# The first MLP product on half the rows: blocks of four F tiles, two tiles side by side in two banks, b1 as a bias of the GELU

## The chip, the core and the metric

The kernel runs on one core of a Trainium2 chip. A core has a matrix engine (PE, with its weight loads shown apart as PEld), a vector engine (DVE), a scalar engine (ACT), a general engine (POOL) and a queue processor (SP) that issues most transfers. They run beside each other, each takes its own instructions strictly in order, and they wait for each other by semaphores. Matmul results go to PSUM, eight banks of 512 fp32 columns for each of 128 partitions. The metric is the device time of one execution in microseconds (us).

## The reference

`x` is 2048 rows of 448 values. The result is `x + s * silu(m)`, with two branches that both start from the layer norm of `x`:

- `s` is a diagonal complex state-space model: inputs go through a complex 448 x 448 matrix, a recurrence over the 2048 rows, and a second complex matrix, plus a skip term.
- `m` is an MLP on a second layer norm: `gelu(y @ w1 + b1) @ w2 + b2`, with `w1` of 448 x 1792 and `w2` of 1792 x 448.

```
def _B_ref(x, w1, b1, w2, b2):
    y = _layernorm(x, axis=-1)
    h = _gelu(jnp.einsum("bsd,df->bsf", y, w1) + b1)
    return jnp.einsum("bsf,fd->bsd", h, w2) + b2
```

All inputs and the output are bf16.

## The kernel before

**Tiling.** The 2048 rows are taken in four groups `g` of 512. A group has two blocks `b` of 256 rows, and in each block the even and the odd rows (`par`) are apart, 128 each. The 1792 columns of `w1` are 14 F tiles of 128, loaded in chunks of 4, 4, 4 and 2 tiles (`CH`). `D` = 448 is three and a half times 128, so the contraction of the first product takes four matmuls for each F tile, the last with 64 rows of `w1` only. The other 64 rows of that last piece hold zeros, but for one row: it holds `b1`, and the transposed input has a 1 in that place. So the product comes with its bias.

**First product.** `mm1` (L686) makes two F tiles for a whole group: 2 x 4 matmuls of 128 x 128 weights on 512 columns, into banks 0 and 1 or banks 2 and 3 by turns; one GELU on ACT (L692) reads both banks, 1024 columns. In group 0, `mm1_half` (L701, GELU L707) does the same for one block at a time, with 256 columns, over three pairs of banks (0-1, 2-3, 4-5). The results, `gT`, are the weights of the second product.

**The rest.** `mm2` (L715) multiplies `gT` by `w2`, 14 matmuls of 448 columns; then DVE adds `b2` (L718), ACT takes Tanh (L719), DVE makes `g_sb` (L720). `bu` (L616) makes the inputs of the recurrence in bank 4, ACT copies them out (L620). `ssm` turns them by tables `WT` (Sin, L553, made once), scans them on DVE (L641), ACT copies the scans to bf16 (L645), DVE turns them back into `h_sb` (L669 to L673). `ym` (L747, L750, L753) multiplies `h_sb`, and for even rows the normalized input too, by the output matrices; DVE multiplies by `g_sb` (L756), adds the skip term (L759), and SP stores. `m0` (L605, L607) and `cq` (L566 to L569) make constant matrices once; `lb` (LB0 to LB6, same lines) makes rows that SP transposes as BT0 to BT6, which `bu` reads. `skips` makes four diagonal matrices De0 to De3; they read the GELU of F tile 4, so that they come after it. `ln_stats`, `ln_scale` and `ln_apply` normalize (xn for the recurrence, xm for the MLP); `xt` transposes, by SP (L83) or, at the start, by PE (L440).

**Order.** Nothing is scheduled at run time. Each helper call adds a task with names that it reads and writes; `link` derives the dependences, buffers and banks by name included. The list `ORDER` gives the order in which tasks are put on their engines' queues, and `SECOND` names the tasks that take their second engine. `emit` puts a wait ahead of a task for each dependence, on its own engine's counter too: a task that adds to a bank which an earlier PE task wrote waits for that one's end.

Of the kernel before, what the change touches and what calls it, by code (L numbers as in the profile page):

```python
# [7 lines left out]
ACT = mybir.ActivationFunctionType  # L8
ALU = mybir.AluOpType
BF = dt.bfloat16  # L10
F32 = dt.float32
# [24 lines left out]
class Plan:  # L36
# [33 lines left out]
    def either(self, first, second, reads=(), writes=(), prio=0.0, chain=False):  # L70

        t = self.add(first[0], first[1], reads, writes, chain=chain)
        t.alts.append((second[0], second[1] if isinstance(second[1], list) else [second[1]]))
        return t
# [72 lines left out]
0 9 18 22 10 1 19 23 11 16 15 12 89 2 20 24 3 8 17 21 14 25 13 5 27 26 7 90 6 28 4 91 29 97 46 92 30 98 31 93 99 32 94 47 100 49 95 33 48 50 96 54 104  # L147
101 34 51 102 55 53 103 56 35 63 106 115 52 36 57 107 117 108 64 116 37 109 65 110 38 66 58 119 118 105 39 59 121 120 67 40 123 146 111 122 112 41 125
145 149 124 147 61 45 143 113 62 148 144 60 182 127 73 126 114 42 150 156 129 155 70 154 128 68 153 69 131 157 130 71 72 161 168 133 83 183 158 77 132
74 160 135 75 170 134 76 84 171 137 78 136 79 159 186 81 174 139 169 80 82 138 175 141 86 87 140 85 312 273 88 162 184 310 152 311 142 309 185 314 315  # L150
313 277 316 274 163 317 164 151 165 281 318 166 319 172 278 320 167 321 322 173 285 323 176 279 177 275 280 178 276 180 234 286 282 287 195 43 369 181
235 179 283 192 288 371 284 370 194 373 44 289 372 292 324 193 325 290 375 293 196 327 374 188 328 399 377 198 376 200 201 294 187 204 379 378 199 291
421 202 425 381 419 380 423 402 420 236 424 382 422 197 426 203 427 383 205 237 206 208 207 209 210 387 532 536 431 384 190 220 385 221 391 432 388
224 386 389 211 428 225 212 222 329 392 228 429 395 223 393 189 213 229 226 394 430 437 227 438 214 433 232 230 238 215 231 191 233 216 529 239 533
531 479 535 217 242 243 240 326 480 244 481 241 252 248 218 482 251 249 434 330 250 435 530 219 485 534 331 247 537 390 254 332 396 245 397 246 253
483 486 268 256 257 262 258 333 541 489 263 542 264 484 267 265 266 259 255 260 269 334 261 538 490 539 487 270 540 335 271 398 272 339 295 488 338
340 491 296 297 346 336 492 348 298 345 337 344 497 436 299 347 343 300 302 350 352 353 498 301 354 355 341 543 356 499 342 357 349 400 493 363 351
509 364 358 500 505 359 544 494 360 361 303 545 362 401 304 495 365 305 496 506 501 366 439 507 367 306 368 508 307 405 403 502 503 504 440 406 404
512 408 441 547 548 407 442 409 546 410 412 411 510 443 607 511 444 413 415 445 449 446 549 416 577 447 448 308 450 579 578 453 458 550 580 457 417
581 513 551 451 610 414 452 418 552 459 582 514 455 468 583 456 553 469 470 454 461 471 472 462 554 463 460 464 465 466 585 467 584 473 555 474 587  # L160
586 475 559 556 588 589 476 477 557 558 478 515 560 590 565 566 595 516 564 517 567 518 596 561 597 562 591 569 519 571 598 520 522 568 521 608 592
563 593 609 599 570 594 523 524 572 603 573 574 600 525 575 601 576 604 616 526 605 602 613 606 527 611 528 617 612 620 614 618 615 628 619 621 624
629 622 630 625 623 626 631 627
""".split()]
SECOND = [int(k) for k in """
44 143 144 148 150 168 172 174 178 180 198 200 204 220 230 232 289 290 317 328 402 404 429 434 435 438 511 512 513 538 539 541 542 544 545 607 611 630
# [12 lines left out]
def bass_recurrent_scan__ssm_conv_s5__mixer_channel_mlp__prompt_kernel(  # L179
# [18 lines left out]
    with ExitStack() as es:  # L198
# [22 lines left out]
        De = SB("De", [128, 4, 128])  # L221
        dbc = SB("dbc", [128, D])
# [51 lines left out]
        with nc.Block():  # L274
# [18 lines left out]
            dve(lambda e: e.memset(w1_sb[64:128, 3, :], 0.0), [], ["w1b"], 0.5, S0)  # L293
            dve(lambda e: e.memset(xn2_sb[:].rearrange("p b (r c) -> p (b r) c", r=2)[:, :, D:512], 0.0), [], XM, 0.1, S0)
            dve(lambda e: e.memset(xn2_sb[:].rearrange("p b (r c) -> p (b r) c", r=2)[:, :, D:D + 1], 1.0), XM, XM, 0.1, S0)
# [21 lines left out]
            def ldw1(c, prio):  # L317
                a, w = CH[c][0] * 128, CH[c][1] * 128
                ld("sp", w1_sb[:, 0:3, a:a + w], dram_ap(B_w1, a, [[F, 128], [128 * F, 3], [1, w]]), [f"w1_{c}"], 384 * w * 2, prio, dur=0.55)
                ld("sp", w1_sb[0:64, 3, a:a + w], dram_ap(B_w1, 384 * F + a, [[F, 64], [1, w]]), [f"w1r_{c}"], 64 * w * 2, prio)  # L320
# [6 lines left out]
            ld("sp", w1_sb[64:65, 3, :], dram_ap(B_b1, 0, [[F, 1], [1, F]]), ["w1b"], 4000, S1 + 1)  # L327
# [8 lines left out]
            ld("pool", b2bc[:], dram_ap(B_b2, 0, [[0, 128], [1, D]]), ["b2bc"], 114688, -50, reads=["sgn3", "w1r_3"])  # L336
# [28 lines left out]
            def first_norm():  # L365

                for par in range(2):
# [9 lines left out]
                    dve(lambda e, src=src, dst=dst, mean=mean, r1=r1: e.tensor_scalar(dst, src, mean, r1, op0=ALU.subtract, op1=ALU.mult),  # L377
# [492 lines left out]
```

## Time and profile before

| | |
|---|---|
| time, median of 3 runs | 160.48 us (159.83 to 160.59) |
| profiled execution, first to last instruction | 159.2 us |
| PE busy | 151.3 us, 95% |
| DVE busy | 136.9 us, 86% |
| ACT busy | 93.2 us, 59% |
| first product: L686, L701 matmuls | 38.2 us (168 of 379 ns), 12.9 us (112 of 273 ns) |
| GELU: L692, L707 | 21.4 us (21 of 1021 ns), 8.3 us (14 of 590 ns) |
| second product: L715 | 43.8 us (224 of 352 ns) |
| scans: L641 | 15.6 us (21 of 784 ns) and 4.4 us (7 of 672 ns) |

The mean time of a matmul in a group row runs from its start to its modelled end, and matmuls overlap; what a matmul costs in a dense row of them is the distance from one to the next, which the chain in order of time gives (a piece's length by its count). A busy time is a share of the span; what a stage is worth is read from the chain of work that ended last, which lists for each moment the instruction or transfer that the end was waiting for. The span is from the first to the last instruction; the time of an execution is a little longer.

### The profile page before, as it was taken

How to read it: one execution, taken by the hardware profiler on the slowest of the kernel's cores; microseconds unless marked ns; L12 is line 12 of the kernel's file. 1: busy time of each engine (PE TensorE's matmuls, PEld its weight loads, DVE VectorE, ACT ScalarE, POOL GpSimd, SP SyncE). 2: the span in 40 equal slices, each digit the busy share in tenths (PEclk: the TensorE clock that was granted, in tenths of full speed). 3: DMA queues.
4: the chain of work that ended last, by engine and by line, in shares of the span. 5: the costliest groups of instructions: out<-in, count | busy, mean ns of one | idle time of the engine just before them, and what ended most of it. 6: DMA issues, size and time to landing. Idle time of an engine off the chain costs nothing.

```text
span 159.2 us, 2725 instructions
## 1 busy us (share of the span) xinstructions
PE 151.3 (95%) x946; PEld 93.7 (59%) x946; DVE 136.9 (86%) x265; ACT 93.2 (59%) x151; POOL 51.5 (32%) x127
## 2 busy tenths in 40 slices
PE   6959999999999999999999999999989999999990
PEld 6849965565565556566655555576556655555560
DVE  5478969999998799999789999893999599999982
ACT  3839899997779962689835472212456972450200
POOL 5578840007616000038600573302015420060021
PEclk9999999999999999999999999999999999999998
DMA  4999999888980057000210430213401000010032
GB/s 103 260 303 364 315 149 198 139 161 159 276 172 4 0 100 147 0 0 4 48 20 0 120 65 1 57 21 94 116 4 58 0 4 0 0 58 0 0 115 60
DMA packets 31174, 14.70 MB, mean 92 GB/s; under 512 B 24693, under 2 KB 30713, under 8 KB 31162
## 3 DMA queue, kind: packets, MB, share of 16 engines
q1 hardware_dynamic: 30914, 14.26, 39.4%
q0 software_dynamic: 96, 0.23, 0.4%
q8 instruction: 7, 0.11, 0.3%
q10 hardware_dynamic: 152, 0.05, 0.1%
q14 instruction: 5, 0.04, 0.1%
HBM read 6.89 MB, written 1.84 MB: 55 GB/s over the span
## 4 chain that ended last, share of the span: by engine, by line
PE 88%; DMA 7%; SPq 2%; DVE 1%; issue 0%
PE psum L715 27%; PE psum L686 21%; PE psum L616 13%; PE psum L747 12%; PE psum L701 7%; PE psum L750 4%; DMA w_sb<-in_B_w_dram 4%; PE psum L605 3%; DMA xnT<-xn_sb 3%; SPq L84 2%; PE psum L753 1%; PE psum L440 0%; DVE t L756 0%; DVE tmp L759 0%; PE psum L607 0%
## 5 line engine op out<-in xcount | busy, mean ns | idle before, releaser
L715 PE MATMUL psum<-w_sb,gT 128*128 128x448 bf16 x224 | 43.8, 352 | 0.0
L686 PE MATMUL psum<-xn2T,w_sb 128*128 128x512 bf16 x168 | 38.2, 379 | 0.1
L715 PEld LDWEIGHTS psum<-w_sb,gT 128*128 128x128 bf16 x224 | 21.9, 98 | 20.0
L692 ACT ACTIVATE gT<-psum 128x1024 bf16<-128x1024 f32 x21 | 21.4, 1021 | 11.7 <-PE psum L686 11.6
L686 PEld LDWEIGHTS psum<-xn2T,w_sb 128*128 128x128 bf16 x168 | 18.5, 112 | 15.8 <-issue 0.7
L616 PE MATMUL psum<-xnT,BT 128*128 128x256 bf16 x196 | 24.0, 273 | 0.5 <-DMA xnT<-xn_sb 0.5
L616 PEld LDWEIGHTS psum<-xnT,BT 128*128 128x128 bf16 x196 | 19.0, 98 | 5.8 <-DMA xnT<-xn_sb 1.0
L719 ACT ACTIVATE th<-o 128x448 f32<-128x448 f32 x16 | 9.1, 573 | 16.4 <-DVE o L718 16.3
L641 DVE TENSOR_TENSOR_SCAN s_f<-cw,cur,v_sb 128x256 f32<-128x256 f32 x21 | 15.6, 784 | 0.2
L701 PE MATMUL psum<-xn2T,w_sb 128*128 128x256 bf16 x112 | 12.9, 273 | 2.0 <-DMA w_sb<-in_B_w_dram 1.8
L701 PEld LDWEIGHTS psum<-xn2T,w_sb 128*128 128x128 bf16 x112 | 11.8, 112 | 2.8 <-DMA w_sb<-in_B_w_dram 2.0
L620 ACT ACTIVATE u_sb<-psum 128x512 bf16<-128x512 f32 x12 | 7.2, 596 | 10.2 <-PE psum L616 10.0
L731 POOL TENSOR_TENSOR xd<-xn_sb,dbc 128x448 bf16<-128x448 bf16 x4 | 4.8, 1198 | 24.9 <-DVE dbc L339 13.9
L747 PE MATMUL psum<-CZ,h_sb 128*128 128x448 bf16 x56 | 11.9, 352 | 0.0
L756 DVE TENSOR_TENSOR t<-psum,g_sb 128x448 bf16<-128x448 f32 (+2 forms) x17 | 9.9, 589 | 1.7 <-PE psum L750 1.1
L358 DVE BATCH_NORM_STATS2 lnst<-x_all 128x6 f32<-128x448 bf16 x14 | 8.2, 611 | 3.5 <-DMA x_all<-in_A_x_dram 3.5
L720 DVE SCALAR_TENSOR_TENSOR g_sb<-th,o 128x448 bf16<-128x448 f32 x16 | 10.4, 664 | 0.7 <-ACT th L719 0.6
L718 DVE TENSOR_TENSOR o<-psum,b2bc 128x448 f32<-128x448 f32 x16 | 9.7, 614 | 1.3 <-PE psum L715 1.3
L747 PE MATMUL psum<-CQ,h_sb 128*128 128x448 bf16 (+2 forms) x54 | 10.5, 332 | 0.0
L731 POOL TENSOR_TENSOR xr<-xd,g_sb 128x448 f32<-128x448 bf16 x5 | 5.5, 1106 | 14.6 <-DVE tmp L759 14.5
L707 ACT ACTIVATE gT<-psum 128x512 bf16<-128x512 f32 x14 | 8.3, 590 | 3.2 <-PE psum L701 2.9
L731 POOL TENSOR_TENSOR xr<-x_all,xr 128x448 f32<-128x448 bf16 x6 | 6.9, 1156 | 9.2 <-DVE xr L732 9.1
(157 smaller groups left out, 224.8 us busy)
## 6 DMA issues: line engine op xcount, KB each, us to landing
out_dram<-tmp SPq DMA_DIRECT2D x7, 224.0 KB, 2.0
w_sb<-in_B_w_dram SPq DMA_DIRECT2D x3, 448.0 KB, 7.0
x_all<-in_A_x_dram SPq DMA_DIRECT2D x3, 448.0 KB, 4.4
w_sb<-in_B_w_dram SPq DMA_DIRECT2D x3, 384.0 KB, 6.2
gT<-in_A_C_re_dram SPq DMA_DIRECT2D x1, 392.0 KB, 11.6
Bn<-in_A_B_re_dram SPq DMA_DIRECT2D x1, 336.0 KB, 6.5
Bn<-in_A_B_im_dram SPq DMA_DIRECT2D x1, 336.0 KB, 6.4
gT<-in_A_C_im_dram SPq DMA_DIRECT2D x1, 336.0 KB, 12.0
```

The lines of the kernel that those rows point to most:

```text
L616: fns = [lambda e, r=r, m=m, d=d: e.matmul(psum[:, 4, r * NK:(r + 1) * NK], BT[:, m, d, :], xnT[:, gx, d, :], start=(d == 0), stop=(d == 6 ...
L641: dve(lambda e, i=i, ri=ri, init=init: e.tensor_tensor_scan(s_f[:, i, ri, :], col(R2, i).to_broadcast([128, NK]), v_sb[:, i, ri, :], init, ...
L686: fns = [lambda e, k=k, d=d: e.matmul(psum[:, b0 + k, :], w1_sb[:, d, fcol(2 * j + k)], rhs[:, d, :, :], start=(d == 0), stop=(d == 3)) fo ...
L692: act(lambda e: e.activation(gT[:, gb, 2 * j:2 * j + 2, :], psum[:, b0:b0 + 2, :], ACT.Gelu_apprx_tanh), [f"ps{b0}", f"ps{b0 + 1}"] + (WK ...
L701: fns = [lambda e, k=k, d=d: e.matmul(psum[:, banks[k], :].rearrange("p (r c) -> p r c", r=2)[:, :, cs], w1_sb[:, d, fcol(2 * j + k)], rhs ...
L715: fns = [lambda e, fi=fi: e.matmul(psum[:, bk, 0:D], gT[:, gb, fi, q * 128:(q + 1) * 128], w2_sb[:, fi, :], start=(fi == 0), stop=(fi == N ...
L718: dve(lambda e: e.tensor_tensor(o2[:, fb, :], psum[:, bk, 0:D], b2bc[:], ALU.add), [f"ps{bk}", "b2bc"], [f"oo{fb}"], 0.62, prio - 76)
L719: act(lambda e: e.activation(th[:, fb, :], o2[:, fb, :], ACT.Tanh, scale=0.5), [f"oo{fb}"] + (WK + WKP if g == 0 else []), [f"th{fb}"], 0. ...
L720: dve(lambda e: e.scalar_tensor_tensor(out=g_sb[:, gs, :], in0=th[:, fb, :], scalar=1.0, in1=o2[:, fb, :], op0=ALU.add, op1=ALU.mult), [f" ...
L731: kb.either(("pool", lambda e, o=o, i0=i0, i1=i1, op=op: e.tensor_tensor(o, i0, i1, op), 1.37, 0.15), ("dve", lambda e, o=o, i0=i0, i1=i1, ...
L747: fns = [lambda e, k=k: e.matmul(psum[:, bk, c0:c1], h_sb[:, hb, k, k0:k0 + 128], cm[:, k, c0:c1], start=(k == 0), stop=False) for k in ra ...
L756: dve(lambda e: e.tensor_tensor(t3[:, fb, c0:c1], psum[:, bk, c0:c1], g_sb[:, gs, c0:c1], ALU.mult), [f"ps{bk}", f"g{gs}"], [f"t3{fb}_{c0} ...
```

## The change

**What is computed how.** The zero rows and the row of `b1` go. The last 64 rows of `w1` are loaded twice, into both halves of the partitions, and the last 64 normalized columns are written twice (`ln_apply`, `first_norm`), so that both halves of the fourth piece hold the same 64 rows. Now an F tile is seven matmuls on 64 rows (three pieces of two halves, and one half of the fourth). `mm1_block` makes a chunk of four F tiles in four banks. A matmul on the low half for tile `k` stands next to one on the high half for tile `k + 1`, which goes to another bank. A pair of tiles is made in two tasks: P1, six matmuls (tile `k` low, `k + 1` high, three pieces), and P2, eight matmuls (`k + 1` low, `k` high, four pieces). In a block the tasks are added as P1 of tiles 0-1, P1 of 2-3, P2 of 0-1 and its GELU, P2 of 2-3 and its GELU. The last chunk, of two tiles, has six whole matmuls and two halves in one task. All chunks of groups 1 to 3 use banks 0 to 3 (the last one banks 0 and 1), and so do those of group 0, whose last chunk uses 4 and 5.

**GELU.** `b1` is loaded as columns (four loads on ACT's queue), copied to fp32 on POOL, and given as the bias of the GELU; since the bias differs by tile, each tile has its own instruction, two in a task.

**Order.** `ORDER` and `SECOND` are new, with 667 tasks for 632. By the tasks' numbers, the parts that the text speaks of are:

- SP, start: x0 even, x0 odd, w1 chunk 0, x1, w1 chunks 1, 2, 3, Bn0, Bn60, both last-rows loads of chunk 0 (`w1r`), Bn1, Bn61, w2 chunk 0, both `w1r` of chunk 3, w2 chunks 1, 2, 3, x2-3, the first load of C (Cn0), both `w1r` of chunk 1, Cn512, transpose BT3, both `w1r` of chunk 2, Cn448, and on as before. (Before: each `w1r` stood right behind its chunk of w1.)
- POOL, start: memset of `ident`, the fp32 copy of b1, the rest of `ident`, constants as before. ACT, start: the four loads of b1, then the four vectors as before.
- PE, group 0: chunk 0 block 0 P1, P1; chunk 3 block 0; chunk 0 P2, P2; transposes; chunk 1 block 0 P1, P1; chunk 3 block 1; chunk 1 P2, P2; chunk 2 block 0 P1, P1; bu; P2, P2; two mm2; chunk 0 block 1 (all four); chunk 1 block 1 P1; bu; m0, m0; bu; m0; chunk 1 P2; bu; P1; m0; bu; P2; chunk 2 block 1 P1, P1, P2; group 1 chunk 0 P1, P2 of tiles 0-1; chunk 2 P2; two mm2.
- ACT, around it: the GELU of chunk 2 block 0 stands behind the scales of `lb`; the first M0 copy behind three `ln_apply` of group 2; the five Sin of `tables` behind the last GELU of group 0, the first Tanh behind them. DVE: De0 and De1 stand behind six of the first nine steps of `tables` and ahead of the other three and of all of `lb` (before: ahead of all of these).
- PE, then: two bu, ym of groups 0 and 1 with one bu between; four bu of group 2; then group 1 chunk 1 P1 (tiles 0-1), chunk 0 P1 (2-3), P2, P2, and after these, for tiles 2-3 alone and each as P1, P2: group 1 chunks 1, 2, group 2 chunks 0, 1, 2; then tiles 0-1 of group 1 chunk 2, chunk 3, and four mm2.
- PE, last: three ym of group 1; four bu; tiles 2-3 of group 3 chunks 0, 1; tiles 2-3 of chunk 2 mixed with tiles 0-1 of group 2 chunk 0; tiles 0-1 of group 2 chunks 1, 2; chunk 3; four mm2; tiles 0-1 of group 3 chunk 0; ym; chunks 1, 2, 3; then mm2 and ym by turns, as before.

The odd rows of `ym` no longer name the transposed input among their reads.

```diff
-            dve(lambda e: e.memset(w1_sb[64:128, 3, :], 0.0), [], ["w1b"], 0.5, S0)
-            dve(lambda e: e.memset(xn2_sb[:].rearrange("p b (r c) -> p (b r) c", r=2)[:, :, D:512], 0.0), [], XM, 0.1, S0)
-            dve(lambda e: e.memset(xn2_sb[:].rearrange("p b (r c) -> p (b r) c", r=2)[:, :, D:D + 1], 1.0), XM, XM, 0.1, S0)
...
-                ld("sp", w1_sb[0:64, 3, a:a + w], dram_ap(B_w1, 384 * F + a, [[F, 64], [1, w]]), [f"w1r_{c}"], 64 * w * 2, prio)
+                for h in range(2):
+                    ld("sp", w1_sb[64 * h:64 * h + 64, 3, a:a + w], dram_ap(B_w1, 384 * F + a, [[F, 64], [1, w]]), [f"w1r{h}_{c}"], 64 * w * 2, prio)
...
-            ld("sp", w1_sb[64:65, 3, :], dram_ap(B_b1, 0, [[F, 1], [1, F]]), ["w1b"], 4000, S1 + 1)
+            for c, (a, n) in enumerate(CH):
+                ld("act", b1c[:, a:a + n], dram_ap(B_b1, a * 128, [[n, 128], [1, n]]), [f"b1c_{c}"], 1000, S1 + 1)
+            pool(lambda e: e.tensor_copy(b1f[:], b1c[:]), [f"b1c_{c}" for c in range(4)], ["b1f"], 0.2, S0)
...
+                parts = [(dst, src)] + ([(xn2_sb[:, b, par * 512 + D:par * 512 + 512], src[:, 384:D])] if which else [])
+                on = [("dve", [lambda e, o=o, i=i: e.tensor_scalar(o, i, rs, nb, op0=ALU.mult, op1=ALU.add) for o, i in parts], 0.4, 0.12),
+                      ("act", [lambda e, o=o, i=i: e.activation(o, i, ACT.Identity, bias=nb, scale=rs) for o, i in parts], 0.75, 0.2)]
...
+            def mm1_block(g, c, b, banks, prio):
+
+                a, n = CH[c]
+                gx = gb = g % 2
+                cols = slice(0, 256) if b is None else slice(b * 128, (b + 1) * 128)
+                rhs = xn2T[:, gx, :, cols].rearrange("p (r d) c -> p d r c", r=2)
+                xk2 = [f"xmT{gx}_{k}" for k in range(2)] if b is None else (["xmT0p0", "xmT0p1"] if b == 0 else ["xmT0_1"])
+                rd = xk2 + [f"w1_{c}"] + [f"w1r{h}_{c}" for h in range(2)]
+
+                def view(k):
+                    return psum[:, banks[k], :].rearrange("p (r c) -> p r c", r=2)[:, :, cols]
+
+                def one(k, d, h, start, stop):
+                    lo, hi = (0, 128) if h is None else (64 * h, 64 * h + 64)
+                    return lambda e: e.matmul(view(k), w1_sb[lo:hi, d, fcol(a + k)], rhs[lo:hi, d, :, :], start=start, stop=stop)
+
+                def evict(k0, prio):
+                    fns = [lambda e, k=k: e.activation(gT[:, gb, a + k, :].rearrange("p (r c) -> p r c", r=2)[:, :, cols], view(k), ACT.Gelu_apprx_tanh,
+                                                       bias=b1f[:, a + k:a + k + 1]) for k in (k0, k0 + 1)]
+                    act(fns, ["b1f"] + [f"ps{banks[k]}" for k in (k0, k0 + 1)] + (WK + WKP if g == 1 else []),
+                        [f"gT{gb}_{a + k}_{q}" for k in (k0, k0 + 1) for q in ((0, 1) if b is None else (b,))], prio=prio, table="gelu")
+
+                for k in range(0, n, 2):
+                    ks = [f"ps{banks[k]}", f"ps{banks[k + 1]}"]
+                    if n > 2:
+                        pe([one(k + h, d, h, d == 0, False) for d in range(3) for h in (0, 1)], rd, ks, prio=prio)
+                    else:
+                        pe([one(k + h, d, None, d == 0, False) for h in (0, 1) for d in range(3)] + [one(k + h, 3, h, False, True) for h in (0, 1)], rd, ks, prio=prio)
+                        evict(k, prio)
+                for k in range(0, n if n > 2 else 0, 2):
+                    ks = [f"ps{banks[k]}", f"ps{banks[k + 1]}"]
+                    pe([one(k + 1 - h, d, h, False, d == 3) for d in range(4) for h in (0, 1)], rd, ks, prio=prio)
+                    evict(k, prio)
...
-                for j in range(7):
-                    mm1_half(j, b, 7 * b + j, 2 * PINNED + 10 + 20 * b + j)
+                for c in range(4):
+                    mm1_block(0, c, b, (0, 1, 2, 3) if c < 3 else (4, 5), 0)
...
-                for j in range(7 if g else 0):
-                    mm1(g, j, pr("mm1", g, j / 10))
+                for c in range(4 if g else 0):
+                    mm1_block(g, c, None, (0, 1, 2, 3), pr("mm1", g, c / 10))
```

## The prediction

> **What bounds the kernel now.** I read the page's shares first, then the chain that ended last, then groups by shape, then the DMA rows.
>
> ```profile
> span 159.2 us, 2725 instructions
> ...
> PE 151.3 (95%) x946; PEld 93.7 (59%) x946; DVE 136.9 (86%) x265; ACT 93.2 (59%) x151; POOL 51.5 (32%) x127
> ...
> PE 88%; DMA 7%; SPq 2%; DVE 1%; issue 0%
> ```
>
> PE is busy 95% of the span and makes 88% of the chain, so any time that PE saves or idles is kernel time. The chain in order of time shows how:
>
> ```profile
> 10.19 3.69 PE psum L701 x32
> ...
> 14.33 7.09 PE psum L701 x64
> 21.42 10.59 PE psum L715 x56
> 32.01 1.53 PE psum L616 x14
> ...
> 33.66 12.26 PE psum L686 x56
> ```
>
> From 10.19 on, PE runs one block after another. A 512-column matmul takes 12.26/56 = 0.219 us here (1.73 per eight, 0.216, elsewhere), a 256-column one 0.109 to 0.111, one of L715 0.189. DVE, at 86%, is nearly as full: it keeps up only because its work lies beside PE's. Next, the evictions and what a per-partition operand costs on ACT (the last two rows have the same shape; only the first takes a column of `sgn`):
>
> ```profile
> L692 ACT ACTIVATE gT<-psum 128x1024 bf16<-128x1024 f32 x21 | 21.4, 1021 | 11.7 <-PE psum L686 11.6
> ...
> L707 ACT ACTIVATE gT<-psum 128x512 bf16<-128x512 f32 x14 | 8.3, 590 | 3.2 <-PE psum L701 2.9
> ...
> L622 ACT ACTIVATE u_sb<-psum 128x256 bf16<-128x256 f32 x4 | 1.5, 380 | 1.5 <-PE psum L616 1.5
> ...
> L553 ACT ACTIVATE WT<-s_f,sgn 128x1024 bf16<-128x1024 f32 x1 | 1.1, 1149 | 0.0
> L544 ACT ACTIVATE s_f<-s_f 128x1024 f32<-128x1024 f32 x1 | 1.0, 1047 | 0.0
> ```
>
> Last, the loads (KB each, us from issue to landing); the timeline of SP has this C load issued at 12.08, as its 22nd.
>
> ```profile
> gT<-in_A_C_re_dram SPq DMA_DIRECT2D x1, 392.0 KB, 11.6
> ...
> w_sb<-in_B_w_dram SPq DMA_DIRECT2D x3, 64.0 KB, 6.0
> ```
>
> **What the edits cost by themselves.** Two tiles take 7 slots for 8 if the halves run side by side: 21 pairs x 0.216 = 4.5 us, and in the first group 14 x (8 x 0.111 - 7 x 0.109) = 1.7: PE's work falls by 6.2. A GELU with a bias costs 590 + 102 = 0.69 us for 512 columns, 380 + 102 = 0.48 for 256; a second starts some 0.09 before the first ends (L425: 0.76 long, 0.67 apart). A pair takes 1.29 or 0.87. The removed memsets (0.81 + 0.17 + 0.06) end before DVE waits for x at 2.4: nothing. The small extra normalization lies between 0.06 (L295) and 0.26 us (L531) on DVE, 0.29 (L374) and 0.40 (L530) on ACT; I take 0.12 and 0.3, nearer the shape. POOL's second task, the copy of b1, waits for four loads on ACT's queue (0.52 + 3 x 0.25 of issue from 0.8, some 2.5 to land, as the Dskip row did at 4.4); behind it stand `ident`, the 28 warm-up matmuls (3.0 us) and the transposes, so xn2T is there at about 9.6. ACT's table load and first normalization move by the same 1.3 us of issue and stay inside it. The load of A, below, covers all this, with 2.4 us to spare for its first block; uncovered, it would cost 3.6. ym's dropped key: nothing, the even rows before it need the same tile. Switches between half and whole arrays: after the four-row matmuls (L460, 4.75) whole ones follow at 4.93, so at most 0.18 each, 31 in the new order, 5.6 in all; I take 0, since four matmuls fill those 0.18.
>
> **What the order does.** The price lies in ORDER. Each engine and SP take their tasks in the order of that list, so I walked it by these durations (the letters are stretches of the new run, P1 and P2 the two parts of a block of the first product, a slot one pass over the columns); a handoff between engines is 0.05 (the chain's "issue" pieces).
>
> A, to 24.0. Both matmul halves of a block read `w1r`, and these loads are no longer next to w1: chunk 0's are the 10th and 11th issues on SP, chunk 1's the 22nd and 23rd, right behind the C load. That slot is issued at 12.1 to 12.6 and lands 11.6 later: 24.0. Lower end 18.4 (the 6.0 row), worth 4.5 in the sum and not 5.6, since the last chunk's block, next on PE, waits for the GELU of its banks until about 20; upper end 26, should the doubled loads' 0.2 MB queue ahead as well. I take 24.0, the row of the same place in the queue. (SP issues three loads more than before, 0.5 each; they are in this count.)
>
> B, to 43.1. PE 17 half slots x 0.109 + 0.16 (end of a matmul, 0.379 - 0.216) and a GELU pair: 2.9. DVE stood all that time at `De0`, which reads that GELU's tile. Behind it: De 0.41, three L542 1.28, a scale 0.45, three L569 1.9, statistics 2.57, ln_scale 2.0, four applies 2.15, LB1 to LB2 1.75: 12.5. Then ACT: two half scales 1.34, GELU pair, u copy 0.5, GELU pair: 3.7. SP is blocked as well: chunk 2's `w1r` stands behind BT3, which waits for LB3 in this list.
>
> C, D, to 60.3. Two L715 groups 5.5. DVE 8.2 (oo, xd, three xn, three scales, two CQ, statistics 3.0), POOL's ln_scale 3.5 (47.23 to 50.73).
>
> E, F, to 81.6. ACT 5.1 (three applies at 0.67 + 0.3, three scales at 0.57, the M0 copy 0.54): PE's second m0 waits for that copy, which stands behind the applies of group 2, and those wait for POOL. Then PE and ACT take turns: two m0, a bu and a P2 4.9; GELU pair and M0 copy 1.4; m0, bu and P2 3.5; three GELU pairs 2.6, for each of which the next part block waits, the part blocks 3.2, handoffs 0.5: 16.2.
>
> G, to 88.0. Sin and Tanh follow the last GELU of the first group: two table loads of 1.28, five Sin 3.83.
>
> H, I, to 122.1. Tanh, g and skip, one after another through ACT, DVE and POOL: 5.9. Then the scans of groups 0 and 1 on DVE with hardly a PE task beside them: 12.7 (3 x 0.95, 6 x 0.61, s_b 1.48, 2 applies 1.1, 4 products 3.5) and 15.5 (the same at 0.68 a scan, with the ym products between). PE's next bu waits for bank 4, whose copy stands behind this on ACT, and ym waits for `h_sb`, the end of the scans.
>
> J, K, to 143.8. ym 2.08; three bu, each waiting for the copy out of the only bank (1.53 + 0.16 + 0.6 + 0.1 = 2.4): 9.3. Then group 2's first products and scans on DVE 8.5, s_b 1.48, and two GELU pairs that stand behind s_b on ACT: 12.4. PE makes two pairs meanwhile and then has no bank.
>
> L, to 165.2. Now the pairs of four chunks follow each other in banks 2 and 3 alone. Each P1 waits for the GELU of the pair before: 7 x 0.216 + 0.21 (P2 waits for the end of P1) + 0.16 + 1.29 + 0.1 = 3.3 for 1.73 before. Four such 13.2, one without 1.75, one more 3.3, the last chunk 3.1.
>
> M, N, to 197.4. Three L715 groups 8.1; o, Tanh, g, four POOL operations at 1.1, then DVE: 10.2, while PE has only ym of group 1 left, whose DVE products stand behind these skip operations in bank 7; ym 2.2; a transpose 3.6, behind ym since it overwrites its tile; four bu 8.1.
>
> O, P, to 240.9. 3.3 + 3.3 + 3.0 + 3.3 + 3.3 + 3.1 = 19.4; four L715 groups 10.6; 1.74 + ym 2.08 + 3.3 + 3.3 + 3.1 = 13.5.
>
> Q, R. Four L715 groups and the eight ym parts, as before: 22.2, to 263.1; last matmul to the end of the span 3.8, as now: 267.
>
> The profiled span is 159.2 and the median 160.48, so 1.3 lie around it: 268.
>
> **Two rules against the trace.** PE's first 28 matmuls went 106 ns apart, the eight transposes at 13.7 (L440) 56 ns apart, and no PE gap after the start is over 1.8 us, so what a longer gap does is not shown. The Trainium skill (TensorE: Matmul & The Clock Gate, HAM oscillation) says that a gap of some 3.4 us brings the half clock back; with about eight such gaps and 3.4 us at half speed after each, an estimate from that page, the sum would be 282. The same skill (TensorEngine Tiling (Array Packing), Key Properties) says that a change of tiling mode drains the engine; it gives no price; the row above bounds it.
>
> **The rivals.** (1) Not slower: the freed PE time counts and the waits don't, because they fall beside other work: 160.5 - 6.2 = 154. It decides if PE's new idle time stays under 6.2 us. Against it: stretch L alone idles 6 x 1.8, and A lets PE's dense part start 13.8 us later. (2) The halves don't overlap: no row shows two half arrays at once. The chain holds 15 full blocks (1.51 each), three halves of the last chunk and about 33 half slots: +27, 295. For it: each half needs its own weight load, and L701's loads take 112 ns beside matmuls 111 apart; against it: L440 loads one every 56 ns. (3) PE is slow after every gap, by the 106 ns row: 3.0 us of such pace after about eight gaps cost 1.5 each, 280. (4) Only the bank waits and the late loads count, and DVE's stretches fall beside PE: 154 + some 17 x 1.8 + (24.0 - 10.2) = 199. Against it: in H and I PE has only two bu and ym, which wait for those scans.
>
> **How the numbers follow.** Forecast 0.70, its own range 250 to 284 (below: A by 4.5, handoffs, DVE rows without overlap; above: extra applies and switches at their upper ends, 5.6 + 4, and part of rival 3). Rival 3 0.11, rival 2 0.12, rival 4 0.05, rival 1 0.02. Leaving out 4 and 1 below and 2 above gives 246 to 292. Faster 0.02, within 0.5% (what a measurement here can tell) 0.01, slower 0.97.
>
> **What would show it.** PE's share falls to some 55% and its slices fall below 5 in the first 45 us and around 95 to 140. Many PE waits name ACT's GELU, about 1.5 us each; DVE's longest wait names the GELU; PE's first waits name w1 loads to about 24 us. Half matmuls start in twos 0.216 apart (if 0.216 singly: rival 2). I am wrong if a queue's order doesn't hold back what I put behind it, or if the loads land in another order than issued.

## The result: 285 us for 160

The changed kernel takes 285.3 us (median of four runs, 284.0 to 286.9). The kernel before, on the same chip, takes 160.2 (159.5 to 160.6). The ratio is 1.784, with a 95% interval of 1.775 to 1.793. The forecast was 268 with a range of 246 to 292. Some runs of a kernel here take over 1.5% longer than its fastest one; the medians below count them, the ratios leave them out.

The page of the changed kernel, its lines that answer to those shown of before (shares, granted clock by fortieths of the span, and the chain by engine):

```profile
span 283.6 us, 3148 instructions
...
PE 182.3 (64%) x1126; PEld 93.6 (33%) x1126; DVE 139.1 (49%) x275; ACT 103.6 (37%) x189; POOL 55.1 (19%) x128
...
PEclk9996659855999755865995599996899999999999
...
PE 47%; DVE 20%; ACT 16%; DMA 5%; issue 4%; SPq 4%; POOL 3%; DVEq 0%; ACTq 0%; POOLq 0%
```

PE was 95% busy and is 64% busy. Its share of the chain falls from 88% to 47%; what comes in is work of DVE, ACT, POOL and SP that lay beside PE before. DVE has the same amount of work (139 us for 137), but the engines now take turns. The clock row is new as well; now it is 5 to 8 in many slices, and before it was

```profile
PEclk9999999999999999999999999999999999999998
```

PE's longest waits in the changed kernel (total us, times, longest):

```profile
PE psum L701 <- ACT gT L704: 28.8, 16, 8.2
PE psum L621 <- ACT u_sb L625: 20.0, 8, 12.0
...
PE psum L701 <- DMA w_sb<-in_B_w_dram: 10.6, 3, 6.6
```

Before, the longest waits of PE were 1.8 and 1.4 us. Twelve of the 16 waits of the first line, 15.6 us, are pairs of F tiles that follow each other in the same two banks; the longest one, 8.2, is the wait ahead of 154.7, for GELUs that stand behind `s_b` on ACT. The chain in order of time shows one such stretch (L of the forecast):

```profile
154.70 1.49 PE psum L701 x6
156.24 1.92 PE psum L701 x8
158.18 1.28 ACT gT L704 x2
159.50 1.49 PE psum L701 x6
161.03 1.91 PE psum L701 x8
162.97 1.27 ACT gT L704 x2
165.39 1.08 PE psum L701 x8
166.49 1.27 ACT gT L704 x2
```

P1 (6 half matmuls), P2 (8), two GELUs, and only then the next P1: the GELUs of two pairs at full clock begin 3.41 apart (166.49, and the next at 169.90), as forecast (3.3). The first two pairs are slower: 1.49 + 1.92 for the same 14 matmuls that later take some 0.86 + 1.07. The granted clock says why (columns: stretch, length, PE busy and its matmuls, clock, DMA share, GB/s):

```profile
103.50:106.70 3.20, 3.16 (x14) 0.50 0.00 0
...
117.00:119.10 2.10, 2.10 (x14) 1.00 0.50 96
121.20:124.30 3.10, 3.10 (x11) 0.69 0.14 57
...
130.20:134.30 4.10, 4.10 (x12) 0.50 0.15 56
154.70:158.20 3.50, 3.37 (x14) 0.50 0.00 0
158.20:163.00 4.80, 3.37 (x14) 0.50 0.01 3
166.50:179.50 13.00, 7.27 (x50) 1.00 0.00 1
```

Behind its long waits PE runs at half clock: a bu takes 3.16 us at 103.5 for 1.53 before.

### The profile page after: what moved, and what is told of

It is laid out like the page before. It is cut to its first block, busy times and chain, and to the rows that moved or that the text cites. A ratio compares the mean times of both kernels' runs of the same rounds, so it can differ in the third digit from the quotient of the medians.

```text
span 283.6 us, 3148 instructions
## 1 busy us (share of the span) xinstructions
PE 182.3 (64%) x1126; PEld 93.6 (33%) x1126; DVE 139.1 (49%) x275; ACT 103.6 (37%) x189; POOL 55.1 (19%) x128
## 3 DMA queue, kind: packets, MB, share of 16 engines
q1 hardware_dynamic: 31232, 14.49, 21.3%
## 4 chain that ended last, share of the span: by engine, by line
PE 47%; DVE 20%; ACT 16%; DMA 5%; issue 4%; SPq 4%; POOL 3%; DVEq 0%; ACTq 0%; POOLq 0%
PE psum L701 16%; PE psum L725 12%; ACT gT L704 9%; PE psum L757 7%; PE psum L621 7%; DVE s_f L646 5%; SPq L84 4%; DMA w_sb<-in_B_w_dram 3%; PE psum L760 2%; DMA xnT<-xn_sb 2%; PE psum L610 2%; DVE xn_sb L429 2%; DVE lnst L361 1%; ACT WT L558 1%; ACT u_sb L625 1%
## 5 line engine op out<-in xcount | busy, mean ns | idle before, releaser
L701 PE MATMUL psum<-xn2T,w_sb 64*128 64x512 bf16 (+3 forms) x460 | 58.2, 374 | 40.4 <-ACT gT L704 28.8
L704 ACT ACTIVATE gT<-psum,b1f 128x512 bf16<-128x512 f32 (+1 forms) x70 | 37.8, 598 | 48.8 <-PE psum L701 48.8
L701 PEld LDWEIGHTS psum<-xn2T,w_sb 64*128 64x128 bf16 (+1 forms) x460 | 25.6, 116 | 72.1 <-issue 35.6
L621 PE MATMUL psum<-xnT,BT 128*128 128x256 bf16 x196 | 31.1, 322 | 24.4 <-ACT u_sb L625 20.0
L757 PE MATMUL psum<-CZ,h_sb 128*128 128x448 bf16 x56 | 15.5, 429 | 5.0 <-DVE t L766 4.5
L639 DVE TENSOR_TENSOR pb<-u_sb,WT 128x1536 bf16<-128x1536 bf16 x4 | 4.7, 1166 | 18.0 <-ACT u_sb L625 18.0
L430 ACT ACTIVATE xn_sb<-x_all,lnw 128x448 bf16<-128x448 bf16 (+1 forms) x14 | 9.1, 685 | 11.5 <-DVE xn_sb L429 9.5
L610 PE MATMUL psum<-CQ,Bn 128*128 128x448 bf16 (+1 forms) x28 | 8.6, 464 | 6.3 <-issue 5.0
L429 DVE TENSOR_SCALAR xn_sb<-x_all,lnw 128x448 bf16<-128x448 bf16 (+1 forms) x30 | 10.7, 398 | 3.7 <-POOL lnw L409 3.0
L757 PEld LDWEIGHTS psum<-CZ,h_sb 128*128 128x128 bf16 x56 | 5.9, 112 | 14.1 <-DVE t L766 6.6
```

The lines of the kernel that those rows point to most:

```text
L429: on = [("dve", [lambda e, o=o, i=i: e.tensor_scalar(o, i, rs, nb, op0=ALU.mult, op1=ALU.add) for o, i in parts], 0.4, 0.12), ("act", [lam ...
L610: fns = [lambda e, k=k, m=m: e.matmul(psum[0:n, bank, 0:D], Bn[:, m, D + d * 128:D + d * 128 + n], CQ[:, k, :], start=(k == 0), stop=False ...
L621: fns = [lambda e, r=r, m=m, d=d: e.matmul(psum[:, 4, r * NK:(r + 1) * NK], BT[:, m, d, :], xnT[:, gx, d, :], start=(d == 0), stop=(d == 6 ...
L701: return lambda e: e.matmul(view(k), w1_sb[lo:hi, d, fcol(a + k)], rhs[lo:hi, d, :, :], start=start, stop=stop)
L704: fns = [lambda e, k=k: e.activation(gT[:, gb, a + k, :].rearrange("p (r c) -> p r c", r=2)[:, :, cols], view(k), ACT.Gelu_apprx_tanh, bia ...
L757: fns = [lambda e, k=k: e.matmul(psum[:, bk, c0:c1], h_sb[:, hb, k, k0:k0 + 128], cm[:, k, c0:c1], start=(k == 0), stop=False) for k in ra ...
```

## The experiments

Times are medians; ratios are against the kernel before in the same series of runs.

| run | what it is | us | ratio, 95% |
|---|---|---|---|
| after | the change | 285.3 | 1.784 (1.775 to 1.793) |
| e1_order | new arithmetic, old order | 168.3 | 1.055 (1.051 to 1.058) |
| e5_oldmm | old arithmetic, new order | 280.2 | four runs, 274.0 to 282.6 |
| e2_loads | change, early loads repaired | 275.7 | 1.715 (1.702 to 1.728) |
| e4_alt | change, bank pairs alternate | 266.2 | 1.666 (1.660 to 1.673) |
| e8_fill | change, pairs moved in among the scans | 263.3 | 1.641 (1.629 to 1.654) |
| e9_warm | change, PE kept running | 278.4 | 1.737 (1.724 to 1.749) |
| e12_first | change, first part in the old order | 260.2 | 1.628 (1.621 to 1.636) |
| e13_rest | change, second part in the old order | 218.7 | 1.369 (1.364 to 1.373) |
| e6_nob1 | e1 without b1 and its GELUs | 165.7 | 1.036 (1.027 to 1.044) |
| e7_bias | before, with b1 as bias | 163.7 | 1.022 (1.015 to 1.030) |
| e10_couple | e6, two pairs together | 169.4 | 1.053 (1.049 to 1.057) |
| e11_best | whole change, repaired | 175.7 | 1.098 (1.092 to 1.104) |

### Order or arithmetic: e1_order and e5_oldmm

The theory was that `ORDER` carries the loss; its rival, that half rows or the split GELU cost it. Each run keeps one of the two.

e1_order, the changed code with the list of before (each task of the old list by its new number, a pair as its two parts):

```diff
-SP: ... w1_1 w1_2 w1_3 Bn.. w1r_0 .. w1r_3 .. Cn0 w1r_1 .. BT3 w1r_2
+SP: ... w1_0 w1r_0 x1 w1_1 w1r_1 w1_2 w1r_2 w1_3 w1r_3 Bn..
-PE: c0 P1 P1, c3, c0 P2 P2, xt, c1 P1 P1, ...
+PE: c0 P1 P2 (tiles 0-1), c0 P1 P2 (tiles 2-3), c1 ..., as mm1_half and mm1 stood
+only c3 of block 1 goes up behind c0 of block 1, since its banks 4-5 are next used by mm2
```

> The half-row matmuls, the doubled loads and the GELU with its bias by tile are all kept; only the order lists go back to those of the kernel before (each last-rows load behind its chunk, each pair of F tiles made in one go where it stood before, pairs alternating between banks 0-1 and 2-3). Theory (the order carries the loss, the arithmetic is a small gain): PE does 6.2 us less work than before, so 160.2 - 6.2 = 154 us; up to 158 us if in group 0 the two GELUs of 0.48 us for each pair (0.96) set the pace against about 0.76 us of PE, 14 x 0.2 = 2.8 us more. Rival (the half-row arithmetic or the split GELU costs by itself, by drained arrays or by ACT): over 165 us, and near 285 us if it is the whole cause.

e5_oldmm, the code of before with the changed list:

```diff
-                b0 = (0, 2, 4)[k3 % 3]
+                b0 = 4 if j == 6 else (j % 2) * 2
 ORDER, SECOND: those of the changed kernel; a pair stands where its P2 stands
```

> The mirror: whole matmuls, one load of the last rows, the row of b1 and one GELU for two tiles, all as in the kernel before, but put in the order of the changed kernel (each pair of tiles where the changed kernel has its second task P2; the first-product banks of group 0 are 0 to 3 and 4-5, as there). Theory (the order carries the loss): a pair in one pair of banks costs 8 x 0.216 = 1.73 of PE, then one GELU of 1.02, against 1.51 and 1.38 in the changed kernel, so the periods are alike (about 3.3 against 3.41 us) and the time is 285 us, from 275 to 290. Rival (the half-row arithmetic and the split GELU are the cause): near the 160 us of the kernel before, under 200.

Measured: 168.3 and 280.2. So the order carries some 117 us of the 125 (285.3 - 168.3), and alone it costs about as much: 280.2 - 159.7 = 120.5 by the median, 114.3 by the shortest of the four runs (274.0). In e5_oldmm whole matmuls (L686) wait for their GELU just as the halves do, by PE's waits:

```profile
PE psum L686 <- ACT gT L692: 19.4, 11, 7.3
```

But e1_order did not reach the 154 to 158 that I had expected; it lost 8.6 us (168.3 - 159.7), as the rival for e1_order had it (over 165). This is the first thing the forecast had wrong, and it was hidden under the large loss.

### The 8.6 us of the arithmetic: e6_nob1, e7_bias, e10_couple

e6_nob1 leaves b1 out of e1_order, so that PE's part (and its doubled loads) stays; e7_bias gives the kernel before the biased GELUs alone.

```diff
 e6_nob1 (against e1_order; b1 is not added)
-                    fns = [lambda e, k=k: e.activation(gT[...a + k...], view(k), Gelu, bias=b1f[:, a + k:a + k + 1]) for k in (k0, k0 + 1)]
+                    fns = [lambda e: e.activation(gT[:, gb, a + k0:a + k0 + 2...], psum[:, banks[k0]:banks[k0] + 2...], Gelu)]
-            the four loads of b1c, the copy to b1f
 e7_bias (against before)
-            ld("sp", w1_sb[64:65, 3, :], dram_ap(B_b1, ...), ["w1b"], ...)
+            the four loads of b1c on ACT's queue, the copy to b1f on POOL
-                act(lambda e: e.activation(gT[:, gb, 2 * j:2 * j + 2, :], psum[:, b0:b0 + 2, :], Gelu), ...)
+                act([lambda e, k=k: e.activation(gT[:, gb, 2 * j + k, :], psum[:, b0 + k, :], Gelu, bias=b1f[:, ...]) for k in range(2)], ...)
```

> Half-row matmuls in the order of the kernel before, as in e1_order, but b1 is left out: its loads and its fp32 copy are gone, and one GELU without a bias takes both tiles of a pair. So what remains of the change is PE's part. In e1_order a pair of 512 columns took 0.79 us for its P1, 0.05 to the start of P2 and 1.05 for P2, with 0.11 more on the next full-row matmuls, about 1.95 us for 1.73 before. Theory now (PE's part is a small loss, as P2 waits for the end of P1 on PE's own counter and each change between half and full rows costs): 21 pairs x 0.1 to 0.2 us: 162 to 164 us. The forecast's term (6.2 us less on PE): 154. Rival (PE's part carries the whole 8.6 us of e1_order): 168.

> The kernel before with whole matmuls and its own order, but b1 as a bias: the load of b1's row is gone (that row stays zero), four loads of b1's columns on ACT's queue and the fp32 copy on POOL are in, and each tile has a GELU of its own. So what remains of the change is ACT's part. Theory: in e1_order the first GELU came at 11.0 us (before: 7.6) since it waits for the copy of b1, 14 pairs took 0.84 instead of 0.59 us on ACT, and the GELU of group 1 began at 41.3 instead of 36.0 us, with PE waiting for it: 160 + 5.3 = 165 us, from 163 to 167. Rival (ACT, 59% busy before, hides its part): 160.

Measured: 165.7 (5.5 more than before, above the 162 to 164 expected) and 163.7 (3.5 more, in its range). The two make 9.0, about the 8.6. Neither part gains, and neither carries it alone. A cut in the middle sorts them: the bu that follows the seven pairs of group 1 starts at 45.92 in the kernel before, and 113.3 us of span are left. It starts at 49.51 in e6_nob1 (115.9 left), at 49.79 in e7_bias (113.2 left), at 51.58 in e1_order (115.3 left). Each figure is of one profiled run, and e6_nob1's took 167.4 us, 1.7 more than its median, so a difference of a microsecond says little.

So the biased GELU costs only at the start. In e7_bias the first GELU begins at 12.18, before at 7.60; in e1_order at 11.02, and its chain goes through the load of b1:

```profile
3.56 5.01 DMA b1c<-in_B_b_dram
9.72 1.28 ACT L704
11.02 0.85 ACT gT L704 x2
```

The table load and the first GELU stand on ACT behind a step that waits for POOL, and POOL stood 5.4 us at the copy of b1. From there on, 14 pairs take ACT 0.84 instead of 0.59 us each.

What e6_nob1 loses ahead of the cut, 3.6 us in this profile, goes through SP by its chain, and not through PE:

```profile
14.38 10.83 DMA x_all<-in_A_x_dram
25.24 2.21 DVE lnst L358 x4
```

With three loads more ahead of it, the load of the rows of group 1 is issued at 14.38, before at 11.60. The statistics wait for it (25.24, before 22.22), DVE's list and the Tanh on ACT follow, and group 1's first GELU begins at 39.44, before at 35.95. So the doubled loads of the last rows cost time in the old order too; no run takes them out alone.

Half rows, for their part, cost behind the cut: 2.0 to 2.6 us more, where the forecast's 0.216 for each of the 14 pairs there had 3.0 less. The chain of e1_order in a stretch of pairs and bu by turns:

```profile
75.60 1.64 PE psum L621 x14
77.24 0.79 PE psum L701 x6
78.07 1.06 PE psum L701 x8
79.13 1.64 PE psum L621 x14
```

From 77.24 a pair and its bu take 3.53 us (to 80.77); before they took 1.73 + 1.53 = 3.26:

```profile
118.72 1.73 PE psum L686 x8
120.45 1.53 PE psum L616 x14
```

Three steps of 0.216 are 0.65, but P1 holds 0.83 until P2 starts, as P2 adds to the same banks and waits for P1's end on PE's own counter; four steps are 0.86, but P2 holds 1.06; and a bu behind half rows takes 1.64 instead of 1.53. In e6_nob1 this own wait is a line by itself among the waits of the weight loads (total us, times, longest):

```profile
PEld psum L698 <- PE psum L698: 13.7, 30, 0.5
```

e10_couple takes it out with e6_nob1's arithmetic:

```diff
 PE
-P1(a) P2(a) | bu | P1(b) P2(b) | bu
+P1(a) P1(b) | bu | P2(a) P2(b) | bu
```

> As e6_nob1 (half rows, no b1, one GELU for a pair, the order of the kernel before; it leaves b1 out), but two pairs of tiles go together: P1 of both, then P2 of both, at the places where the two pairs stood (where a bu stood between them, it stands between the P1s and the P2s). So no P2 waits any more for a P1 directly ahead of it, and there are no more changes between half and full rows than before. In e6_nob1 30 of PE's weight loads waited for PE itself, and P1 took 0.79 + 0.05 us where three steps of 0.216 are 0.65. Theory (the wait of P2 for P1 is the larger part of what half rows lose on PE): 18 waits in groups 1 to 3 x 0.2 = 3.6 us off 165.7: 162 us, from 160.5 to 163. Rival (the changes of rows are the loss, or GELU waits come in the place): 165 to 167.

Measured: 169.4, more than e6_nob1 (the intervals of the two ratios don't overlap), where 162 was expected, and above the 165 to 167 of the rival too. The own wait shrinks, and GELU waits (the rival's second form) and a load wait are new, by the waits of PE and of its weight loads in e10_couple (the profiled run took 170.7 us, the shortest 167.9).

```profile
PE psum L698 <- ACT gT L701: 5.7, 9, 1.9
...
PEld psum L698 <- PE psum L698: 4.4, 6, 1.2
...
PE psum L722 <- DMA w_sb<-in_B_w_dram: 3.0, 1, 3.0
```

With two pairs in four banks, the next P1 finds no free bank until a GELU is through. But by the cut used above the loss stands ahead of it: that bu starts at 53.33 (e6_nob1: 49.51), behind the load of `w2` in the last line and, by the chain, behind SP's transposes of C, and 115.3 us are left (115.9). So behind the cut couples are about even, and which of these causes takes the gain that was expected is not shown.

The halves themselves keep their pace in a dense row: here 12 half matmuls take 1.42 us and 16 take 1.85 (pieces of e11_best's chain, which has the same couples): 0.216 for each two, and some 0.12 at the end.

### Where the order loses: e12_first and e13_rest

The list was cut behind the last second product of group 0 (which ends at 91.5 us in the changed kernel), and one side of it put in the order of e1_order.

```diff
 e12_first
-ORDER[:316] of the changed kernel
+the same tasks in the sequence of e1_order
 e13_rest
-ORDER[316:] of the changed kernel
+the same tasks in the sequence of e1_order
```

> The changed kernel with the first part of its order alone replaced: all tasks up to group 0's last second product (which ends at 91.5 us in the changed kernel) stand in the order of e1_order, all later ones as they are in the changed kernel. Theory (the loads, the list of DVE ahead of De0, and the turns of PE and ACT in group 0 are a third of the loss): that part has some 37 us of PE work from 11 us on and 10 to 15 us of waits for the constant matrices, so it ends near 62 us instead of 92: 285 - 30 = 255 us, from 247 to 262. Rival (only the late loads count there, the rest is hidden by DVE): 275, as in e2_loads.

> The mirror of e12_first: the changed kernel up to group 0's last second product, and all later tasks in the order of e1_order. Theory: behind 92 us PE has 20 pairs at 1.95 us (39), 12 second products (32), bu (14.5) and ym (27), 112 us, and is the bound again: 92 + 112 + 4 = 208 us, from 203 to 220, so that this part of the order carries some 77 us. Rival (DVE's scans, which start no earlier than 99 us, bound the rest): DVE has 92 us of work behind that point, and with its waits the time is over 225.

Measured: 260.2 (25 less than the changed kernel) and 218.7 (67 less). Both lie in their ranges. In e12_first the first step of group 0's scans (the turn by `WT`) starts 23 us earlier; the row of the changed kernel's chain, and of e12_first's timeline:

```profile
99.43 1.71 DVE pa L638
```
```profile
76.01 1.79 DVE L638 TENSOR_TENSOR pa<-u_sb,WT 128x1536 bf16<-128x1536 bf16 x1
```

The two gains sum to 92 of the 117 us. The other 25 need both sides: in e1_order the seven pairs of group 1 are made ahead of 51 us, while the constants and transposes are still under way, and the cut leaves them behind it. In e12_first PE stands idle there (6.72 us for a transpose at 40 to 46.7, and 5.01 ahead of its first m0, as in the changed kernel). That they make up the whole 25 is argued, not shown.

### Single causes within the new order: e2_loads, e4_alt, e8_fill, e9_warm

```diff
 e2_loads, SP and POOL alone
-SP: w1_0 x1 w1_1 w1_2 w1_3 ... w1r_0 ... w1r_3 ... w1r_1 ... w1r_2
+SP: w1_0 w1r_0 x1 w1_1 w1r_1 w1_2 w1r_2 w1_3 w1r_3 ...
-POOL: ident, b1f, ident, constants
+POOL: ident, ident, constants, b1f
```

> The changed kernel with its early queues alone repaired: on SP both last-rows loads of a chunk directly behind that chunk's load, on POOL the fp32 copy of b1 behind the other constants. Nothing else moves. Theory: the first-product tasks that waited to 21.7 us (chunk 1) and 33.2 us (chunk 2) no longer wait for loads; the first is 8 to 9 us earlier (PE's first product starts at 13.0 us), and what follows goes by the list on DVE and the transposes behind it, so 285 - 9 = 276 us, from 271 to 281. Rival 1 (the loads only cover another wait: the list on DVE ahead of De0 and the order of ACT set the same end): 283 to 287. Rival 2 (the loads start most of the loss, as everything after runs in order and cold): under 262.

Measured: 275.7, as expected (276): the late `w1r` and the early copy of b1 on POOL, which this run undoes together, cost 9.6 us. The changed kernel's chain goes through the `w1r` loads, and not through POOL; the part that they stand in, with the transposes and the cold bu behind them:

```profile
12.33 8.91 DMA w_sb<-in_B_w_dram
21.68 4.07 PE psum L701 x28
...
34.87 3.21 DMA xnT<-xn_sb
38.32 3.15 PE psum L621 x14
```

```diff
 e4_alt, PE from the middle of group 1 on (ACT's GELUs follow)
-g1 c1, c2, g2 c0, c1, c2 (all tiles 2-3, banks 2-3), then g1 c2, c3 (banks 0-1)
+tiles 2-3 and 0-1 by turns, P1 and P2 of a pair together
```

> The changed kernel with one thing undone: from the middle of group 1 on, the pairs of F tiles are made alternately in banks 2-3 and 0-1, instead of all pairs of banks 2-3 in a row and then all of banks 0-1, and a pair's P1 and P2 stand together; the GELUs on ACT follow in the same sequence. The number of tasks and the rest of the order stay. Theory (a pair's matmuls, then its GELUs, then the next pair of the same banks make 3.41 us where 1.51 us of PE and 1.38 us of ACT could overlap): some 17 of the 22 pairs after 154 us gain 3.41 - 1.6 = 1.8 us each, 31 us at most, less what the scans on DVE and the transfers take in their place, so 260 us, from 254 to 268. Rival (DVE's scans or the second product set these stretches anyway): over 275.

Measured: 266.2, near the upper end. PE's waits for the GELU fall from 28.8 us in 16 to 12.8 us in 5; the gain is 19 us of the 31 at most.

```diff
 e8_fill, PE (ACT's GELUs likewise)
-mm2 mm2 bu bu ym bu ym ym ym ym bu bu bu bu | nine pairs | mm2 ...
+mm2 mm2 pair bu pair bu pair pair ym pair bu ym pair ym pair ym pair ym pair bu bu bu bu | mm2 ...
```

> The changed kernel with nine pairs of the first product (the rest of group 1, and tiles 2-3 of group 2's first three chunks), which stand behind the scans of groups 0 and 1 on PE and ACT, moved in front of and between them (between the bu and the ym there). Theory (PE idles while DVE scans, 99 to 130 us, and DVE idles while PE makes these pairs, 155 to 180 us with 0.4 us of DVE work): the 24.8 us of the second stretch go, 285 - 25 = 260 us, from 256 to 266. Rival (their GELUs on ACT delay the copies that the scans and ym wait for, so the scans' stretch grows by as much): over 275.

Measured: 263.3, 22 us less (theory 25). PE's work and DVE's scans do fit beside each other; the changed order had put them one behind the other.

```diff
 e9_warm, PE (banks 7 and 5 are free there; no result reads these)
+pe([lambda e: e.matmul(psum[:, bank, 0:128], ident, ident, start=True, stop=True)] * n, ["ident"], [bank])
+n = 180 behind mm2, 50 behind the first bu, 30, 34 and 8 behind three ym of group 0
```

> The changed kernel with 302 matmuls of 128 columns that no result reads (180, 50, 30, 34 and 8 of them), put on PE into its waits between 91 and 130 us, so that PE does not stand still there. Theory (part of the time above the forecast is PE at a lower clock behind its waits: the granted clock is 0.61 from 99 to 130 us and 0.76 in the 12 us behind, where bu takes 2.35 to 3.15 us instead of 1.53 and an ym of 11 matmuls 4.28 instead of 2.08): bu and ym there come back to their full pace, 2.6 us in the scans' stretch and 2.9 behind it: 285 - 5 = 280 us, from 277 to 282, and the clock of that stretch is over 0.9. Rival (the lower clock lies beside DVE's scans and costs nothing): 284 to 287.

Measured: 278.4, 6.9 us less. The same stretch of the scans, of the changed kernel and then of e9_warm (length, busy times of PE, PEld, DVE, ACT and POOL, then the clock, DMA share and GB/s):

```profile
99.40:130.20 30.80, 17.56 (x72) 8.48 (x72) 28.94 (x47) 11.26 (x21) 13.01 (x24) 0.61 0.10 23
```
```profile
99.40:130.20 30.80, 21.86 (x220) 15.75 (x218) 27.58 (x46) 9.65 (x19) 11.65 (x23) 1.00 0.12 31
```

So more work on PE made the kernel faster: the lower clock lies on the path. 1.7 us of the difference stand ahead of the first of these matmuls in the two profiles (the table load for Sin starts at 84.28 instead of 85.99), so some 5 are theirs, as expected.

The gains of these four runs sum to 58 us (9.6, 19.1, 22.0 and 6.9). No run undoes them together, and no run sorts the rest of the 117 by single causes; e12_first and e13_rest only say on which side of 91.5 us it lies.

### The whole change, repaired: e11_best

```diff
+e1_order's list with the couples of e10_couple
-                for h in range(2):
-                    ld("sp", w1_sb[64 * h:64 * h + 64, 3, a:a + w], ..., [f"w1r{h}_{c}"], ...)
+                ld("sp", w1_sb[0:64, 3, a:a + w], ..., [f"w1r0_{c}"], ...)
+            ld("act", w1_sb[64:128, 3, :], dram_ap(B_w1, 384 * F, [[F, 64], [1, F]]), [f"w1r1_{c}" for c in range(4)], ...)
+            ld("act", b1c[:, 0:12]..., ["b1c_0"], ...); ld("act", b1c[:, 12:14], ..., ["b1c_3"], ...)
+            act(lambda e: e.activation(b1f[:], b1c[:], ACT.Copy), ...)
```

> The whole change, put as well as the runs so far suggest: half rows in couples as in e10_couple, the order of the kernel before elsewhere, b1 loaded first on ACT's queue in two loads and copied on ACT just ahead of the first GELU, and the second copy of the last rows in one load on ACT's queue, so that SP has fewer loads than before. Theory (after the order and the loads are repaired, what stays is ACT's two GELUs for a pair in group 0, 14 x 0.25 = 3.5 us, with PE's part about even): 160.2 + 3.5 = 163.7, from 161.5 to 165. Rival (with the waits gone the half rows gain at last): under 159.5.

Measured: 175.7, worse than e1_order, and both theory and rival fall. Its chain starts with the one large load on ACT's queue (issued at 3.40, landed 5.72 later, so PE's first pair starts at 9.17 and the first GELU at 12.87), and PE waits 14 times for a GELU, 8.5 us in all. By the cut used above it is behind e1_order on both sides: the bu starts at 55.47 (51.58), and 117.8 us are left (115.3). How much of this is the couples, whose GELUs are longer here than in e10_couple, and how much the large load or the transposes of C, which stand on its chain too, is not shown. No version of the change that was run beats the kernel before.

## Why the prediction was right, and where it was wrong

The sign and the place were right. The price was put on the order, by walking each queue, and the time (285.3) lies in the range. It lies above the forecast's own 250 to 284, though, and only in the wider range that allows for the rivals; and misses of both signs cancel in it (A came 2.3 us early), so that its nearness is in part luck. By stretches (boundaries from the chain of the changed kernel): C and D took 17.8 us for 17.2 forecast, G 6.6 for 6.4, K 12.35 for 12.4, M and N 33.2 for 32.2, O 19.8 for 19.4, P 24.7 for 24.1, Q 22.3 for 22.2. (Two sums were 0.1 off: the terms of O make 19.3, the last ones of F 16.1.) The larger misses are E and F, 23.5 for 21.3, H to J, 49.8 for 43.4, and these steps; with them the last instruction came 16.6 us later than forecast:

- **A, 24.0 forecast, 21.7 measured.** The wait was the right one (`w1r` of chunk 1); its load landed 8.9 us after issue, not 11.6 (that was the row of a load of 392 KB; this one has 64). Its cover for b1 had less to spare than thought: POOL stood 5.7 us for b1, and PE's first product started at 13.0, where the forecast had its input at 9.6.
- **B, 19.1 forecast, 23.0 measured.** The list of DVE did follow De0, which waited 5.0 us, but it wasn't the end: behind DVE's statistics the chain goes through a transpose by SP (34.87 to 38.08; chunk 2's `w1r`, landed at 33.2, is off the chain), and the bu behind it ran at half clock (3.15 for 1.53).
- **The clock, taken as nothing in the likeliest case (rival 3).** This is the main miss. On the chain of the changed kernel a bu takes 3.15 (1.53), an m0 2.79 (1.32), one ym 2.79 + 1.49 and another 2.79 + 1.08 (2.08), two pairs of L 3.4 each (1.94), one bu 2.35, and ym pieces of the scans' stretch 2.31 and 2.42 (1.32 and 1.14): 1.6 + 1.5 + 2.2 + 1.8 + 2.9 + 0.8 + 1.0 + 1.3 = 13 us beside the 16.6 (those in B and L are in these bullets too). e9_warm tests the 5.3 us of them that lie from 113 to 137 us, and gained about 5; the other 7.8 are argued from the clock there (0.50, and 0.57 in the second ym). Rival 3 had 12 us for it and a chance of 0.11; it is no rival at all but an addition to the forecast, since the waits that the forecast itself listed bring it about. With the estimate from the Trainium skill (TensorE: Matmul & The Clock Gate, HAM oscillation: no gap of PE over some 3.4 us) it would have been 282. The trace agrees that the clock halves behind long waits (the 0.50 in the rows above) and e9_warm that it costs time; on the length of the gap the trace differs, as the last section shows.
- **The edits by themselves, -6.2 forecast, +8.6 measured (e1_order).** "PE's work falls by 6.2" is the step that failed: PE is busy for 155.4 us in e6_nob1 and for 151.3 before, both at full clock. P2's wait for P1 was in the sum for L (0.21) but not for the other places where a pair stands alone. The change of modes, taken as 0 under a bound of 0.18, costs 0.11 where full rows follow halves. And b1's path to the first GELU was covered by A only in the new order; uncovered, it was named at 3.6, and e7_bias measured 3.5 for it and the split GELU together. The three loads more on SP were counted in A alone; in the old order they hold back the load of group 1's rows (some 3 us in e6_nob1's profile). In the number this hardly showed (285.3 against e5_oldmm's 274.0 to 282.6, where the arithmetic is the old one), but rival 1's 154 was not to be had even in the old order: the whole arithmetic took 168.3 there. The durations of the GELU (0.69 and 0.48 forecast) were right: 0.684 and 0.469.
- **L, 21.4 forecast, 24.8 measured.** The chain of banks was right (3.3 a pair forecast, 3.41 measured); what is over is the two cold pairs.

Rival 2 (the halves don't overlap) is refuted: 16 half matmuls take 1.85 us, where 16 single ones would take 3.46. Rival 4 (only bank waits and loads count) is refuted by e13_rest and e8_fill: DVE's stretches no longer lie beside PE, and it matters.

Of what the forecast wanted to see: PE's share is 64% and not 55%, for PE was busy longer at the lower clock; PE's waits for the GELU in L are 1.36 to 1.56 us each (forecast 1.5); PE's first wait, of 7.2 us, names POOL, whose constants stand behind the copy of b1, and the loads of `w1` follow up to 21.7 us. DVE's longest wait does not name the GELU: that one (De0) is 5.0 us, while DVE waited up to 27.3 us for the second product.

## What to carry to other kernels

When a diff brings a new hand-made order together with new arithmetic, cost them apart, and run them apart: here the order carried 117 of 125 us, and it hid that the arithmetic loses too. A matmul count that falls by an eighth is worth nothing if each pair pays an own wait (0.2 us), a change of rows (0.1) or a bank that waits for its eviction, or if its extra loads hold back others in the queue; count these before the gain. And if a forecast lists waits of PE, add the slow pace behind them to the same sum.

## What the hardware showed that I had not expected

The granted clock can fall to half behind a wait of 2.0 us: between 119.1 and 121.2 PE stood still, worked at full clock for about a microsecond, and then ran at 0.50 (0.57 from 122.2 to 123.4). The length of the last wait does not decide it alone, for in e9_warm PE stood three times for 2.0 to 2.2 us (ahead of 101.85, 108.52 and 112.24), and the clock was 1.00 throughout. It comes back late: from 154.7 to 163.0, 8.3 us with 6.7 us of PE work in them, it stayed at 0.50, with a wait of only 1.36 us between. And a filler helps: with matmuls that nothing reads in the waits, the clock of the whole stretch was 1.00.
